# Ten units routed first, fourteen later, in a fused RWKV and mixture-of-experts kernel on one core

## The chip, the core and the metric

The kernel runs on one NeuronCore of a Trainium2 chip. The core has four compute engines that work side by side, each through its own queue in order: TensorE (PE, matrix products; PEld is its weight load), VectorE (DVE), ScalarE (ACT) and GpSimd (POOL). SyncE (SP) issues transfers. POOL can also issue an indirect transfer, which scatters the rows of a tile to row numbers held in another tile. The metric is device time in microseconds (us) of one execution, lower is better; a time is the median of several executions.

## What is computed

Attention first: a recurrence over 768 steps for 4 batches and 8 heads of size 48. Its output, 3072 rows of 384 numbers, goes through a mixture of 8 experts of which each row uses one.

```python
# attention, for each step t
cur = np.einsum('bhd,bhe->bhde', u[None] * kt, vt)
y[:, :, t] = np.einsum('bhd,bhde->bhe', rt, state + cur)
state = wt[:, :, :, None] * state + np.einsum('bhd,bhe->bhde', kt, vt)
# experts, x is y as (3072, 384)
logits = x @ w_gate + modality_bias[modality_id]
e_idx = np.argmax(logits, axis=1)
probs = softmax(logits); gate_w = probs[np.arange(N), e_idx]
h = np.maximum(x[mask] @ w1[e], 0.0)          # mask = e_idx == e
out[mask] = gate_w[mask, None] * (h @ w2[e])
```

The bias has a spread of 0.5 and the attention output is small, so in the given inputs nearly every row goes to the expert that the bias of its modality favours.

## The kernel before

**Attention.** The 3072 rows are 24 units of 128 rows (`NU`). One call of `att_iter(i)` is a turn; the loop at the end of the program runs i from -2 to 23. In turn i, DVE scans the decays of unit i+2 (`B`, `E`, L261 and L264) and masks the scores of unit i+1 (`A`, L303); POOL computes `dV` of unit i, `K` and `G` of unit i+2 (L268, L219, L272); PE makes the scores of unit i+1 (`pS`, L302) and the output of unit i (`pY`, L327 and L337). `x_rows` writes a finished unit to the tile `xp`, `x_cols` transposes it, and `logits` (L376) puts its 8 logits for each row into columns of `R`, one PSUM tile that also holds all scratch of the routing. Steps of setup and routing are put in a list, `hooks`; each turn takes one, after the logits of the turn and ahead of the matmuls of `pY`, but in turns 22 and 23 the logits are emitted after the hook, among or behind the matmuls of `pY`.

**Routing.** Units 0 to 11 are routed in turns 13 to 18 (`route_a`, `route_x`, `route_b`, then three steps of `table`). `route_a` finds the expert of each row, `route_b` counts ranks by matmuls and writes each row's place to `posT`; `scatter(n)` is then POOL's indirect write of unit n to `xs` in DRAM, where rows stand sorted by expert. `drain(2)` issues two of them behind each turn. `table` works out, for the first `NA` = 5 blocks of 256 rows, the expert, the place in `xs`, and whether the weights change. Units 12 to 23 are routed in blocks 0 and 1, written in blocks 2 and 3, and the second table holds the other `NB` = 7 blocks and halves.

**Blocks.** Weights of the expert that the bias favours (`e0`) are loaded and split in advance (`w_split_half`, POOL and ACT, turns 8 to 15). Each block q loads its rows by `blk_load` (SP, L576), which waits for all writes to `xs`; `blk_t` transposes them and splits them into `xh` and `xo` (L587 to L589); `blk_up` makes four groups of products with w1, `blk_down` four with w2, `blk_out` scales by the gate and writes the rows with POOL's indirect transfer (L627). `blk_t` of the next block stands in PE's queue between the ups and the downs of the present one. `w_split` splits the weights of the next block: w1 (DVE, ACT) in the ups, w2 (POOL, ACT) in the downs. `fetch` issues the load of block q+2 at the end of block q, for blocks from `NA` on; the loads of the first `NA` are issued in turn 21. Weights are loaded by a conditional transfer (`blk_raw`, L196), which moves nothing where the expert stays. Twelve blocks and one half block are laid out in the program; loops behind them take what overflows.

**Order.** The schedule is manual: each engine runs its instructions in the order in which the code emits them. What one engine writes and another reads or overwrites is guarded by semaphores that the framework places.

## Time and profile before

| | |
|---|---|
| median of 3 runs | 367.51 us (367.09 to 367.93) |
| the profiled execution | 367.16 us |
| its span, first to last instruction | 365.3 us |
| mean granted TensorE clock | 0.995 |
| PE, PEld busy | 349.1 us (96%), 334.6 us (92%) |
| DVE, ACT, POOL busy | 226.7 us (62%), 224.5 us (61%), 247.6 us (68%) |
| HBM traffic | 239 GB/s over the span |

Busy shares are means over two stages: the attention turns up to about 133 us, and the expert blocks behind them. PE's records are pipelined, so a busy PE is not PE at its peak. In a timeline row stand the start, the duration, the engine, the line, the operation with the tiles that it writes and reads, and, in brackets, the idle time ahead of it and what ended that.

### The profile page before, as it was taken

How to read it: one execution, taken by the hardware profiler on the slowest of the kernel's cores; microseconds unless marked ns; L12 is line 12 of the kernel's file. 1: busy time of each engine (PE TensorE's matmuls, PEld its weight loads, DVE VectorE, ACT ScalarE, POOL GpSimd, SP SyncE). 2: the span in 40 equal slices, each digit the busy share in tenths (PEclk: the TensorE clock that was granted, in tenths of full speed). 3: DMA queues.
4: the chain of work that ended last, by engine and by line, in shares of the span. 5: the costliest groups of instructions: out<-in, count | busy, mean ns of one | idle time of the engine just before them, and what ended most of it. 6: DMA issues, size and time to landing. Idle time of an engine off the chain costs nothing.

```text
span 365.3 us, 10829 instructions
## 1 busy us (share of the span) xinstructions
PE 349.1 (96%) x4245; PEld 334.6 (92%) x4245; DVE 226.7 (62%) x356; ACT 224.5 (61%) x466; POOL 247.6 (68%) x221
## 2 busy tenths in 40 slices
PE   7899999999898999999999999999999999999993
PEld 2788988998777999999999999999999999999992
DVE  6899999999998827671578390707161626661110
ACT  3665677677355538564586768686768585854340
POOL 5658868989798907856878867474747474728271
PEclk9999999999999999999999999999999999999998
DMA  8976887787795260012255613131222664065200
GB/s 283 330 200 196 247 217 230 229 233 214 199 282 167 70 216 1 2 45 65 108 184 188 209 52 109 50 104 57 96 72 82 185 234 154 20 215 155 81 26 26
DMA packets 20128, 53.28 MB, mean 146 GB/s; under 512 B 2693, under 2 KB 12587, under 8 KB 20068
## 3 DMA queue, kind: packets, MB, share of 16 engines
q1 hardware_dynamic: 16932, 43.04, 39.0%
q0 software_dynamic: 3136, 9.47, 6.9%
q8 instruction: 35, 0.57, 0.7%
q14 instruction: 25, 0.20, 0.2%
HBM read 75.66 MB, written 11.63 MB: 239 GB/s over the span
## 4 chain that ended last, share of the span: by engine, by line
PE 79%; DVE 9%; issue 6%; POOL 2%; ACT 1%; DMA 1%; POOLq 0%; DVEq 0%; ACTq 0%
PE pS_u L602 20%; PE pY_d L619 14%; PE pX_d L619 14%; PE pT_u L602 9%; PE pS L302 5%; PE pY L337 4%; PE pY L327 3%; DVE B L261 3%; DVE A L303 2%; PE pK L286 2%; PE pU_st L313 2%; DVE R L216 2%; PE pR_x L376 2%; PE pT L243 2%; PE pK_x L587 2%
## 5 line engine op out<-in xcount | busy, mean ns | idle before, releaser
L202 POOL TENSOR_TENSOR wl<-raw,wh 128x768 fp32r<-128x768 f32 x52 | 96.7, 1868 | 70.7 <-ACT wh L201 70.5
L201 ACT CAST wh<-raw 128x768 fp32r<-128x768 f32 x96 | 79.3, 830 | 34.1 <-PE pX_d L619 24.4
L602 PE MATMUL pS_u<-xh,wh 128*128 128x256 f32 x198 | 56.4, 285 | 0.0
L602 PE MATMUL pS_u<-xo,wh 128*128 128x256 f32 x198 | 55.9, 282 | 0.0
L602 PE MATMUL pS_u<-xh,wl 128*128 128x256 f32 x198 | 55.6, 281 | 0.0
L608 DVE SCALAR_TENSOR_TENSOR hl<-pS_u,hh 128x512 fp32r<-128x512 f32 x33 | 22.8, 690 | 52.7 <-ACT hh L607 51.2
L202 DVE TENSOR_TENSOR wl<-raw,wh 128x768 fp32r<-128x768 f32 x44 | 48.2, 1096 | 3.0 <-ACT wh L201 1.9
L627 POOL DMA_INDIRECT out<-ot,xl x25 | 32.6, 1302 | 10.9 <-ACT ot L626 5.3
L602 PEld LDWEIGHTS pS_u<-xh,wl 128*128 128x128 f32 x198 | 37.5, 190 | 0.0
L602 PEld LDWEIGHTS pS_u<-xh,wh 128*128 128x128 f32 x198 | 37.2, 188 | 0.0
L602 PEld LDWEIGHTS pS_u<-xo,wh 128*128 128x128 f32 x198 | 37.2, 188 | 0.0
L607 ACT ACTIVATE hh<-pS_u 128x512 fp32r<-128x512 f32 x33 | 19.7, 597 | 27.6 <-PE pS_u L602 22.9
L608 DVE SCALAR_TENSOR_TENSOR hl<-pT_u,hh 128x512 fp32r<-128x512 f32 x15 | 10.3, 690 | 40.8 <-ACT hh L607 40.3
L225 ACT ACTIVATE pU_st<-pU_st,B 128x48 f32<-128x48 f32 x80 | 22.0, 275 | 19.6 <-PE pU_st L313 13.8
L619 PE MATMUL pY_d<-wh,hh 128*128 128x384 f32 x96 | 33.6, 350 | 0.0
L619 PE MATMUL pY_d<-wh,hl 128*128 128x384 f32 x96 | 32.6, 339 | 0.0
L619 PE MATMUL pX_d<-wl,hh 128*128 128x384 f32 x96 | 32.6, 339 | 0.0
L619 PE MATMUL pX_d<-wh,hl 128*128 128x384 f32 x96 | 32.5, 338 | 0.0
L619 PE MATMUL pX_d<-wh,hh 128*128 128x384 f32 x96 | 32.5, 338 | 0.0
L619 PE MATMUL pY_d<-wl,hh 128*128 128x384 f32 x96 | 32.4, 338 | 0.0
L268 POOL TENSOR_TENSOR dV<-v,dT 128x384 f32<-128x384 f32 x24 | 20.0, 834 | 18.1 <-ACT dT L245 14.1
L303 DVE TENSOR_TENSOR A<-pS,cs 128x1024 f32<-128x1024 f32 x24 | 29.2, 1217 | 3.9 <-PE pS L302 2.0
(182 smaller groups left out, 899.6 us busy)
## 6 DMA issues: line engine op xcount, KB each, us to landing
raw<-w SPq DMA_DIRECT2D x52, 768.0 KB
in<-rkw SPq DMA_DIRECT2D x20, 674.2 KB
xl<-xs SPq DMA_DIRECT2D x12, 386.0 KB
v<-vt SPq DMA_DIRECT2D x24, 192.0 KB
wg<-wf SPq DMA_DIRECT2D x8, 576.0 KB
raw<-w SPq DMA_DIRECT2D x16, 192.0 KB
xs<-zt SPq DMA_DIRECT2D x8, 193.0 KB
in<-rkw SPq DMA_DIRECT2D x3, 512.0 KB
```

The costliest lines, as they stand in the source:

```text
L201: nc.scalar.copy(out=wh[k][:, sl], in_=raw[k][:, sl])
L202: (nc.vector, nc.gpsimd)[k].tensor_tensor(out=wl[k][:, sl], in0=raw[k][:, sl], in1=wh[k][:, sl].bitcast(F32), op=ALU.subtract)
L225: nc.scalar.activation(out=st[:, p], in_=st[:, p], func=AF.Copy, scale=tot[:, p, 0:1])
L268: nc.gpsimd.tensor_tensor(out=dV, in0=T["v", z].rearrange("p (a b) -> p a b", a=H), in1=T["dT", z].rearrange("p a b -> p (a b)")[:, :, Non ...
L302: nc.tensor.matmul(out=pS[:, hh, p], lhsT=K[q, p], rhs=R[q, p], start=True, stop=True)
L303: nc.vector.tensor_tensor(out=A.rearrange("p a b c -> p (a b) c"), in0=pS.rearrange("p a b c -> p (a b) c"), in1=mask[:, None, :].to_broad ...
L337: nc.tensor.matmul(out=pY[q:q + 64, h * D:(h + 1) * D], lhsT=A[:, hh, p, q:q + 64], rhs=v[:, h * D:(h + 1) * D], start=(first(z) and h == ...
L602: nc.tensor.matmul(out=pp[:, i], lhsT=wsrc[0][:, f, c * P:(c + 1) * P], rhs=xsrc[:, c], start=(n == 0), stop=(n == 3 * KC - 1))
L607: nc.scalar.activation(out=hh, in_=pp, func=AF.Relu)
L608: nc.vector.scalar_tensor_tensor(out=hl, in0=pp, scalar=0.0, in1=hh.bitcast(F32), op0=ALU.max, op1=ALU.subtract)
L619: nc.tensor.matmul(out=X["y", q][j], lhsT=hsrc[:, i, j * P:(j + 1) * P], rhs=wsrc[1][:, f], start=(f == 0 and n == 0), stop=(f == FC - 1 a ...
L627: ins = nc.gpsimd.indirect_dma_start(out=out[:, :], out_offset=bass.IndirectOffsetOnAxis(ap=xl[:, j, DM + 1:DM + 2].bitcast(I32), axis=0), ...
```

## The change

Units 0 to 9 are routed in turns 11 to 13 and units 10 to 23 in blocks 0 and 1 (`CUT`, `NJS`, `part`). `NA` becomes 4 and `NB` 8. Block 0 takes its expert and the place of its rows from `e0` (a new tile `e0r`), no longer from the table; its 256 rows are filled with padding first (a new transfer in turn 6), and the table takes off one block of that expert (`oh0`, `hd`). The first table's steps run in turns 22 and 23, two in each. `drain` issues one write a turn from turn 13 on, and two in turn 21, there between `K` and `G`. Only block 0 is loaded in turn 21, blocks 1 to 3 behind the last turn. Fourteen later writes go out in blocks 1 and 2; the second table's steps, the second `hook_b` and the padding rows move ahead by about a block. The bias is added to the logits by a matmul into `R` (`mfx`, `rbx`; one matmul with a start flag clears the tile first), so `route_a` has two operations fewer. The reciprocal of the gate's sum moves from `route_b` to `blk_t` and `half_t`. Sixteen half splits of w1 come ten in turns 8 to 12, three in turn 22 and three behind turn 23.

```diff
--- before.py
+++ after.py
@@ -28,8 +28,8 @@
 BT = 256
-NA = 5
-NB = 7
+NA = 4
+NB = 8
@@ -44,7 +44,8 @@
-NJ = 2 * NCH
+CUT = (0, 10, NU)
+NJS = (CUT[1], NU - CUT[1])
@@ -142,10 +143,16 @@
     e0f = cp.tile([P, 1], F32, name="e0f")
...
+    mfx = cp.tile([64, P], F32, name="mfx")
+    rbx = cp.tile([64, NU, E], F32, name="rbx")
+    mi2 = cp.tile([64, 2 * P], I32, name="mi2")
+    oh0 = cp.tile([P, E], F32, name="oh0")
+    e0r = cp.tile([P, 1], I32, name="e0r")
         nc.sync.dma_start(out=bb, in_=bass.AP(bias.tensor, bias.offset, [[0, P], [1, 2 * E]]))
         nc.sync.dma_start(out=mi, in_=mid)
+        nc.sync.dma_start(out=mi2[32:32 + NU], in_=mid)
     mf = raw[1][0:NU, 0, 0:P]
@@ -160,6 +167,12 @@
         nc.scalar.copy(out=mf, in_=mi[:, 0:2 * P:2])
         nc.scalar.copy(out=ersb[0:1], in_=ers[0:1])
         nc.scalar.copy(out=rcol(C_VEC + 3 * E, 1), in_=zt[:, 0:1])
+        nc.scalar.copy(out=mfx[0:NU], in_=mi[:, 0:2 * P:2])
+        nc.scalar.activation(out=mfx[32:32 + NU], in_=mi2[32:32 + NU, 0:2 * P:2], func=AF.Copy, scale=-1.0, bias=1.0)
+        for s in range(2):
+            q = slice(32 * s, 32 * s + NU)
+            nc.gpsimd.tensor_tensor(out=rbx[q], in0=ident[q, q, None].to_broadcast([NU, NU, E]),
+                                    in1=bb[q, None, (1 - s) * E:(2 - s) * E].to_broadcast([NU, NU, E]), op=ALU.mult)
@@ -172,14 +185,17 @@
     def setup_b():
-        pm = rcol(C_VEC, NU)
+        pm = T["pT", 5][:, 400:400 + NU]
         nc.tensor.transpose(out=pm, in_=mf, identity=ident[0:NU, 0:NU])
+        nc.tensor.matmul(out=T["R"][:, 0:NU * E], lhsT=mfx, rhs=rbx.rearrange("p a e -> p (a e)"), start=False, stop=True, skip_group_check=True)
         nc.scalar.copy(out=m1[:, 1], in_=pm)
         nc.gpsimd.tensor_scalar(out=m1[:, 0], in0=m1[:, 1], scalar1=-1.0, scalar2=1.0, op0=ALU.mult, op1=ALU.add)
         bias_part(0, biasT)
         nc.vector.tensor_reduce(out=e0f, in_=ec.rearrange("p a e -> p (a e)"), axis=AX.X, op=ALU.min)
+        nc.vector.tensor_scalar(out=oh0, in0=i8, scalar1=e0f[:, 0:1], scalar2=None, op0=ALU.is_equal)
         nc.gpsimd.tensor_scalar(out=e0f, in0=e0f, scalar1=float(E), scalar2=None, op0=ALU.add)
         nc.gpsimd.tensor_copy(out=e0i, in_=e0f)
+        nc.gpsimd.tensor_scalar(out=e0r, in0=e0f, scalar1=float(RS), scalar2=None, op0=ALU.mult)
@@ -248,7 +264,7 @@
     hooks = []
     done = iter(range(2 * FC))
-    SPLITS = {i: 2 for i in range(8, 16)}
+    SPLITS = {**{i: 2 for i in range(8, 13)}, 22: 3}
     def att_iter(i):
         a, m, z = i + 2, i + 1, i
@@ -269,6 +285,8 @@
                                     in1=T["dT", z].rearrange("p a b -> p (a b)")[:, :, None].to_broadcast([P, H, D]), op=ALU.mult)
         if ok(a):
             mk_k(a, k)
+            if i == NU - 3:
+                drain(2)
             nc.gpsimd.tensor_tensor(out=wt(a, "G", [P, 512]), in0=r, in1=k, op=ALU.mult)
         for _ in range(SPLITS.get(i, 0)):
             w_split_half(next(done))
@@ -352,29 +370,33 @@
...
     def x_rows(n):
...
-        if n % NJ == 0:
-
-            T["xp", b // 2] = (rt if b else xa).tile([P, NJ, XW], F32, tag="xp", name=f"xp{b}", bufs=1)
...
         if j == 0:
-            T["xb", b] = T["xp", b // 2][:, b % 2 * NCH:(b % 2 + 1) * NCH]
+
+            T["xp", c] = (rt if c else xa).tile([P, NJS[c], XW], F32, tag="xp", name=f"xp{c}", bufs=1)
         if n == 0:
             T["R"] = pt("x", "pR")
-        nc.vector.tensor_tensor(out=T["xb", b][:, j, 0:DM], in0=T["pY", n][:, 0:DM],
+
+            nc.tensor.matmul(out=T["R"][:, 511:512], lhsT=wm[:, 0:P], rhs=wm[:, 0:1], start=True, stop=True, skip_group_check=True)
+        nc.vector.tensor_tensor(out=T["xp", c][:, j, 0:DM], in0=T["pY", n][:, 0:DM],
                                 in1=T["dV", n].rearrange("p a b -> p (a b)"), op=ALU.add)
+    def part(n):
+        c = n >= CUT[1]
+        return int(c), n - CUT[c]
+
...
     def logits(n):
...
                 nc.tensor.matmul(out=T["R"][q:q + 64, n * E:(n + 1) * E], lhsT=T["xT", n][:, c * P + q:c * P + q + 64], rhs=wgs[:, c],
-                                 start=(c == 0), stop=(c == KC - 1), skip_group_check=True)
+                                 start=False, stop=(c == KC - 1), skip_group_check=True)
@@ -395,57 +416,58 @@
...
     def route_a(c):
...
-        nc.vector.scalar_tensor_tensor(out=lg, in0=lg, scalar=-1.0, in1=biasT[:, c * NJ:(c + 1) * NJ], op0=ALU.mult, op1=ALU.subtract)
...
-        nc.vector.tensor_reduce(out=mx, in_=lg, axis=AX.X, op=ALU.min)
-        nc.vector.tensor_tensor(out=eq, in0=lg, in1=mx[:, :, None].to_broadcast(sh), op=ALU.is_equal)
...
+        nc.vector.tensor_reduce(out=mx, in_=lg, axis=AX.X, op=ALU.max)
         nc.vector.tensor_tensor(out=lg, in0=lg, in1=mx[:, :, None].to_broadcast(sh), op=ALU.subtract)
         yield
-        nc.vector.tensor_tensor(out=eq, in0=eq, in1=i8[:, None, :].to_broadcast(sh), op=ALU.mult)
+        nc.vector.scalar_tensor_tensor(out=eq, in0=lg, scalar=0.0, in1=i8[:, None, :].to_broadcast(sh), op0=ALU.is_equal, op1=ALU.mult)
         nc.vector.tensor_reduce(out=ix, in_=eq, axis=AX.X, op=ALU.min)
...
         nc.vector.tensor_tensor(out=oh, in0=i8[:, None, :].to_broadcast(sh), in1=ix[:, :, None].to_broadcast(sh), op=ALU.is_equal)
         if c:
...
                 nc.vector.tensor_reduce(out=ohs, in_=T["oh", 0].rearrange("p a b -> p b a"), axis=AX.X, op=ALU.add)
-        nc.gpsimd.tensor_copy(out=T["xp", c][:, :, DM + 1:DM + 2].bitcast(I32), in_=tidi[:, c * NJ:(c + 1) * NJ, None])
+        nc.gpsimd.tensor_copy(out=T["xp", c][:, :, DM + 1:DM + 2].bitcast(I32), in_=tidi[:, CUT[c]:CUT[c + 1], None])
     def route_x(c):
...
-        nc.scalar.activation(out=ex, in_=rcol(c * NE, NJ, E), func=AF.Exp, scale=-1.0)
...
+        nc.scalar.activation(out=ex, in_=rcol(CUT[c] * E, NJS[c], E), func=AF.Exp)
         for n in (4, 2, 1):
             nc.gpsimd.tensor_tensor(out=ex[:, :, 0:n], in0=ex[:, :, 0:n], in1=ex[:, :, n:2 * n], op=ALU.add)
-        nc.gpsimd.tensor_scalar(out=ex[:, :, 0:1], in0=ex[:, :, 0:1], scalar1=1.0e-9, scalar2=None, op0=ALU.add)
+        nc.gpsimd.tensor_scalar(out=T["xp", c][:, :, DM:DM + 1], in0=ex[:, :, 0:1], scalar1=1.0e-9, scalar2=None, op0=ALU.add)
     def route_b(c):
...
-        add(pR[:, 0:NE], trib, oh.rearrange("p a b -> p (a b)"), True)
+        add(pR[:, 0:NE], trib, oh.rearrange("p a b -> p (a b)"), c == 1)
...
         if c:
...
-
-        for j in range(NJ):
-            add(pR[:, (j + 1) * E:], onesb, oh[:, j:j + 1].to_broadcast([P, NJ - j, E]), stop=j == NJ - 1)
...
+
+        for j in range(nj):
+            add(pR[:, (j + 1) * E:], onesb, oh[:, j:j + 1].to_broadcast([P, nj - j, E]), stop=j == nj - 1)
...
         nc.vector.tensor_tensor(out=rk, in0=rk, in1=oh, op=ALU.mult)
...
             nc.vector.tensor_reduce(out=po, in_=rk, axis=AX.X, op=ALU.add)
-        nc.vector.reciprocal(out=T["xp", c][:, :, DM:DM + 1], in_=T["ex", c][:, :, 0:1])
@@ -453,7 +475,7 @@
         vec, tt, ts = nc.vector, nc.vector.tensor_tensor, nc.vector.tensor_scalar
-        ct = rcol(C_RK + NE, E)
+        ct = rcol(C_RK + NJS[ph] * E, E)
...
@@ -492,7 +514,7 @@
             ts(out=es, in0=te, scalar1=float(E - 1), scalar2=None, op0=ALU.min)
             ts(out=tab[:, 0, o:o + nb], in0=te, scalar1=float(E - 1), scalar2=None, op0=ALU.min)
-            prev = e0f if o == 0 else tabe[:, o - 1:o] if o == NA else tabe[:, NQ - 1:NQ]
+            prev = e0f if o == 1 else tabe[:, o - 1:o] if o == NA else tabe[:, NQ - 1:NQ]
             for c0, c1, pv in ((0, 1, prev), (1, nb, es[:, 0:nb - 1])):
                 vec.scalar_tensor_tensor(out=tab[:, 2, o + c0:o + c1], in0=te[:, c0:c1], scalar=float(E - 1), in1=pv,
                                          op0=ALU.min, op1=ALU.not_equal)
@@ -502,12 +524,16 @@
...
         if ph == 0:
             rounded(g, ct, 1.0 / BT, -0.5 + 0.5 / BT)
+            hd = wt(ph, "hd", [P, E], 1)
+            tt(out=hd, in0=g, in1=oh0, op=ALU.min)
+            tt(out=g, in0=g, in1=hd, op=ALU.subtract)
             sums(cu, g)
-
-            ts(out=fs, in0=cu, scalar1=float(NA), scalar2=None, op0=ALU.min)
-            vec.scalar_tensor_tensor(out=fA, in0=cu[:, 1:E + 1], scalar=float(NA), in1=fs[:, 0:E], op0=ALU.min, op1=ALU.subtract)
             yield
-            yield from rows(0, NA, cu, fA, None)
+
+            ts(out=fs, in0=cu, scalar1=float(NA - 1), scalar2=None, op0=ALU.min)
+            vec.scalar_tensor_tensor(out=fA, in0=cu[:, 1:E + 1], scalar=float(NA - 1), in1=fs[:, 0:E], op0=ALU.min, op1=ALU.subtract)
+            yield from rows(1, NA - 1, cu, fA, hd)
+            tt(out=fA, in0=fA, in1=hd, op=ALU.add)
...
         vec.scalar_tensor_tensor(out=n, in0=fA, scalar=-float(BT), in1=ct, op0=ALU.mult, op1=ALU.add)
@@ -572,12 +598,13 @@
     def blk_load(q, at=None):
         at = q if at is None else at
         xl = bp["m"].tile([P, JT, XW], F32, tag="xl", name=f"xl{q}", bufs=5)
-        r = nc.sync.value_load(tab[0:1, 1, ds(at, 1)], min_val=0, max_val=DUMMY)
+        r = nc.sync.value_load(e0r[0:1, 0:1] if q == 0 else tab[0:1, 1, ds(at, 1)], min_val=0, max_val=DUMMY)
         nc.sync.dma_start(out=xl, in_=xs[ds(r, BT), :].rearrange("(j p) c -> p j c", p=P))
         X["xl", q] = xl
     def blk_t(q):
         xl = X["xl", q]
+        nc.vector.reciprocal(out=xl[:, :, DM:DM + 1], in_=xl[:, :, DM:DM + 1])
         xh = bp["m"].tile([P, KC, BT], F32R, tag="xh", name=f"xh{q}", bufs=2)
         for c0, c1, tg in ((0, 2, "pK"), (2, 3, "pU")):
@@ -639,6 +666,8 @@
         X["xl", q] = xl
     def half_t(q):
+        xl = X["xl", q]
+        nc.vector.reciprocal(out=xl[:, 0:1, DM:DM + 1], in_=xl[:, 0:1, DM:DM + 1])
         pp = pt(f"x{q}", tag="pK", sh=(P, KC, P))
         for c in range(KC):
             nc.tensor.transpose(out=pp[:, c], in_=X["xl", q][:, 0, c * P:(c + 1) * P], identity=ident)
@@ -682,9 +711,9 @@
     def hook_b(c):
...
-        pend.extend(range(c * NJ, (c + 1) * NJ))
-
-    for t, c in (*((t, 0.0) for t in SPb), (onesb, 1.0), (one8, 1.0), (ersb, 0.0), (zt, 0.0), (zt[:, DM + 1:DM + 2].bitcast(I32), PAD_ID),
+        pend.extend(range(CUT[c], CUT[c + 1]))
+
+    for t, c in (*((t, 0.0) for t in SPb), (onesb, 1.0), (one8, 1.0), (ersb, 0.0), (zt, 0.0), (zt[:, DM:DM + 1], 1.0), (zt[:, DM + 1:DM + 2].bitcast(I32), PAD_ID), (mfx, 0.0), (rbx, 0.0),
                  (glo, W_LO), (ghi, -W_HI)):
         nc.gpsimd.memset(t, c)
@@ -692,14 +721,18 @@
         if 6 <= i < 6 + 2 * FC:
             if i == 6:
                 e0 = nc.sync.value_load(e0i[0:1, 0:1], min_val=0, max_val=E - 1)
+                r0 = nc.sync.value_load(e0r[0:1, 0:1], min_val=0, max_val=(E - 1) * RS)
+                nc.sync.dma_start(out=xs[ds(r0, BT), :].rearrange("(j p) c -> p j c", p=P), in_=zt[:, None, :].to_broadcast([P, JT, XW]))
             w_raw(e0, (i - 6) // FC, (i - 6) % FC, parts=FC)
         if 3 <= i < 7:
             hooks.append((setup_a, setup_b, setup_c, setup_d)[i - 3])
-        if i == NJ + 1:
+        if i == CUT[1] + 1:
             ra, tb = route_a(0), table(0)
-            hooks.extend([lambda: next(ra), lambda: next(ra, None), lambda: hook_b(0), *[lambda: next(tb, None)] * 3])
-        if i == NJ + 2:
+            hooks.extend([lambda: next(ra), lambda: next(ra, None), lambda: hook_b(0)])
+        if i == CUT[1] + 2:
             route_x(0)
+        if i >= NU - 2:
+            hooks.append(lambda: [next(tb, None) for _ in range(2)])
         if i == NU - 1:
         att_iter(i)
@@ -713,15 +746,14 @@
         if i == 0:
             early()
-        drain(2)
-        if i == 19:
-            blk_raw(0, 0)
-            blk_raw(0, 1)
-        if i == 21:
-            for q in range(NA):
-                blk_load(q)
+        if i < NU - 3:
+            drain(1)
+        if i == NU - 3:
+            blk_load(0)
     assert not pend and not hooks
     blk_raw(1, 0)
+    for q in range(1, NA):
+        blk_load(q)
@@ -758,12 +790,15 @@
                 else:
                     logits(NU - 4 + g)
                 w_split(1, g)
-            if (q, g) == (1, 0):
-                route_x(1)
             if nxt < HO and g < late:
                 w_split(0, g)
-            if q in (2, 3):
+            if (q, g) == (1, 0):
+                hook_b(1)
+                tab1 = table(1)
+            if (q, g) > (1, 1):
                 drain(1)
+            if (q, g) == (2, 1):
+                next(tab1, None)
         if q == 0:
             blk_raw(1, 1)
         (blk_t if nxt < HO else half_t)(nxt)
@@ -771,26 +806,26 @@
             blk_raw(nxt2, 0)
         if 1 <= q <= NG:
             guard_load(q - 1)
-        if q == 1:
-            hook_b(1)
-        if q == 2:
-            tab1 = table(1)
         for g in range(FC // 2):
             blk_down(q, g)
             if q == 0 and g < FC // 2 - late:
                 w_split(0, late + g)
             w_split(1, g)
-            if q == 0 and g == FC // 2 - late:
+            if q == 0 and g == 0:
                 list(route_a(1))
+            if q == 0 and g == 1:
+                route_x(1)
             if g == 1 and 2 <= q <= NG + 1:
                 guard(q - 2)
-            if q == 2:
+            if q in (1, 2):
                 drain(1)
-
-            if (q, g) in ((2, 0), (2, 1), (2, 2), (3, 0), (3, 2)):
+            if q == 1:
                 next(tab1, None)
-            if (q, g) == (2, 0):
-                pad_rows()
+        if q == 1:
+            pad_rows()
+        if q == 2:
+            assert not pend
+            next(tab1, None)
         if q == 0:
             blk_raw(2, 0)
         if q == NG + 1:
```

## The prediction

> **What bounds the kernel now.** I read the chain of waits by engine first, then the windows by stage, then the timelines around the routing work. Times are on the before-trace's own clock.

> ```profile
> span 365.3 us, 10829 instructions
> PE 79%; DVE 9%; issue 6%; POOL 2%; ACT 1%; DMA 1%; POOLq 0%; DVEq 0%; ACTq 0%
> ```
> ```profile
> 76.40:110.00 33.60, 30.90 (x671) 27.83 (x670) 32.49 (x62) 19.36 (x59) 29.39 (x35) 1.00 0.81 232
> 207.40:340.00 132.60, 132.60 (x952) 132.44 (x952) 60.40 (x82) 90.89 (x143) 80.04 (x48) 1.00 0.36 117
> ```

> The columns after a stretch are its length and the busy time of PE, PEld, DVE, ACT and POOL. In the expert blocks (207.4 to 340 stands for them) PE is never idle: a microsecond of PE idleness there is a microsecond of span. In the attention turns (76.4 to 110) DVE is busy 32.49 of 33.60 us and POOL 29.39: there work taken from DVE or POOL shortens the span. So the change can win ahead of the blocks and lose wherever it makes PE wait.

> The seeded inputs, run through the reference, put 1336 of the first twelve units' rows on expert 1 (five full blocks), 1110 of the first ten's (four), 2663 and 409 of all on experts 1 and 6. Both kernels then run twelve blocks and one half with the same weight switches. No matmul of a block is saved.

> **Part 1, attention turns: -3.3 us.**

> ```profile
> 48.78 1.21 DVE L303 TENSOR_TENSOR A<-pS,cs 128x1024 f32<-128x1024 f32 x1
> 68.55 1.22 DVE L303 TENSOR_TENSOR A<-pS,cs 128x1024 f32<-128x1024 f32 x1
> 78.13 1.21 DVE L303 TENSOR_TENSOR A<-pS,cs 128x1024 f32<-128x1024 f32 x1
> 79.86 0.26 DVE L406 SCALAR_TENSOR_TENSOR pR_x<-pR_x,biasT 128x96 f32<-128x96 f32 x1
> 80.92 1.22 DVE L261 TENSOR_TENSOR_SCAN B<-in,pX_d 128x516 f32<-128x516 f32 x1
> 127.29 1.22 DVE L303 TENSOR_TENSOR A<-pS,cs 128x1024 f32<-128x1024 f32 x1 [0.90 <-PE pS L302]
> ```
> ```profile
> 98.77 1.01 POOL L558 DMA_INDIRECT xs<-xp,posT  x1 [0.17 <-DVE B L261]
> 100.08 0.97 POOL L558 DMA_INDIRECT xs<-xp,posT  x1 [0.30 <-issue]
> 104.45 1.00 POOL L558 DMA_INDIRECT xs<-xp,posT  x1 [0.17 <-issue]
> ```

> One A per turn: 48.78 is turn 7, 68.55 turn 11, 78.13 turn 13, 127.29 turn 22. Turns 7 to 13 take 29.35/6 = 4.89 us, turns 11 to 13 DVE's bare 4.79; turns 11 to 22 take 58.74/11 = 5.34. The excess has two causes. Four routing operations add 80.92 - 79.86 = 1.06 to a DVE that has no gap. And with two indirect writes POOL needs 104.45 - 98.77 = 5.68 a turn; one write is 1.31 of it, so the new turn needs 4.37, below DVE's 4.79. After the change eleven turns at 4.79 to 4.89 make 52.7 to 53.8, I take 53.3. What stays is two, three and two routing operations in turns 11 to 13, 7 x 0.23 = 1.6 (0.265 each for 96 columns, less for 80). 54.9 against 58.74 saves 3.8. From it goes what the bias costs in setup:

> ```profile
> 31.81 0.30 ACT L160 CAST raw<-mi 24x128 f32<-24x128 int32 x1
> ```

> The two new ACT copies are of this kind and stand ahead of a dT for which PE waits; pipelined, 0.2 each, they cost 0.4 (0 to 0.6), the bias matmul about 0.1. Net -3.3; ends -4.9 (all at 4.79, setup hidden) and -2.2 (a slow write or two as below).

> **Part 2, the table in the last two turns: +4.2 us.**

> ```profile
> L376 PEldq EVENT_SEMAPHORE  x6: 51/51/51, 82.5 to 111.1; - x6
> 128.36 0.47 PE L376 MATMUL pR_x<-cs,xT 128*64 128x8 f32 x12
> 133.17 0.49 PE L376 MATMUL pR_x<-cs,xT 128*64 128x8 f32 x12
> 133.59 0.39 PE L602 MATMUL pS_u<-xh,wh 128*128 128x256 f32 x1
> ```
> ```profile
> 102.60 0.20 DVE L474 TENSOR_TENSOR pR_x<-pR_x,cs 128x40 f32<-128x40 f32 x1
> 103.63 1.23 DVE L261 TENSOR_TENSOR_SCAN B<-in,pX_d 128x516 f32<-128x516 f32 x1
> 108.44 0.16 DVE L490 SCALAR_TENSOR_TENSOR pR_x<-pR_x,t2(0, 0)_1984 128x5 f32<-128x5 f32 x1
> 108.98 1.22 DVE L261 TENSOR_TENSOR_SCAN B<-in,pX_d 128x516 f32<-128x516 f32 x1
> 132.66 0.41 DVE L589 TENSOR_TENSOR xo<-pU_x,xh 128x256 fp32r<-128x256 f32 x1
> ```

> The first row decides. PE holds an extra wait ahead of the logits (L376) six times, from 82.5 to 111.1: turns 14 to 19, each the turn behind one of the six hooks in which DVE worked in the tile R. The logits write other columns of R than those hooks touch. So PE's writes to R stand behind DVE's earlier work on R, whatever the columns. Before, that cost nothing: the hook came behind its turn's logits and the next were a turn away. In turns 22 and 23 the code puts the logits behind the hook. Turn 22's hook is now 17 DVE operations (5 to the first yield, 12 to the second); five took 103.63 - 102.60 = 1.03, so 17 take 3.5. They start 1.14 after A (127.29), end 4.7 after it; the logits stood at 128.36, 1.07 after it: PE stalls 3.6. Turn 23's hook has 7: six took 0.54 and the last needs 0.15 to finish, so it ends 0.65 behind xo (133.07), at 133.7 against logits at 133.17: 0.6 more. Behind the waiting logits in PE's queue stand pY, delta, block 0's transposes and all blocks. Ends: 17 x 0.09 (the short six) gives 2.1 in all, 17 x 0.265 gives 5.1.

> [...]

> **Part 3, block 0's load: 0, behind part 2.**

> ```profile
> 126.56 5.67 SPq L576 DMA_DIRECT2D xl<-xs  x5
> 130.74 0.66 PE L587 MATMUL pK_x<-cs,xl 128*128 128x128 f32 x4
> 131.54 0.88 PE L327 MATMUL pY<-SPb,R 128*64 128x96 f32 x16
> 204.71 0.97 POOL L558 DMA_INDIRECT xs<-xp,posT  x1 [0.30 <-issue]
> 207.51 0.39 SPq L576 DMA_DIRECT2D xl<-xs  x1
> 208.50:210.50 2.00, 2.00 (x19) 2.00 (x18) 0.30 (x1) 1.69 (x4) 2.00 (x2) 1.00 0.73 198
> ```

> SP issues a load 2.80 after the start of the last write (204.71 to 207.51), and that load's traffic is over by 210.5: 3.0 more. (The load of 126.56 was there by 130.74, so at most 4.2; 1.0 passes before anything moves.) The two writes of turn 21 now go out between K and G, the second starting near 124.6; its load would be ready near 130.4 to 131.4 where PE wants it at 130.74. With PE 3.6 late it is hidden. If PE did not wait for the table, 1.1 would show: DVE's x_rows, 0.5 behind the table's end at 132.0, would release pY at 132.6 in place of 131.54.

> **Part 4, block 4's load: +5.3 us.** This is the price of routing fourteen units and four early blocks: the first load that waits for later writes is now issued one block earlier, with two writes more ahead of it.

> ```profile
> SPq L576 <- DMA xs<-xp,posT: 14.6, 2, 9.5
> 166.49 1.83 POOL L202 TENSOR_TENSOR wl<-raw,wh 128x768 fp32r<-128x768 f32 x1 [5.59 <-ACT wh L201]
> 184.98 1.85 POOL L202 TENSOR_TENSOR wl<-raw,wh 128x768 fp32r<-128x768 f32 x1 [2.12 <-ACT wh L201]
> 187.99 1.88 POOL L202 TENSOR_TENSOR wl<-raw,wh 128x768 fp32r<-128x768 f32 x1
> 198.25 0.44 PE pK_x L587 x4
> ```

> SP waited for these writes twice, once ahead of each batch of loads. Before, the late load was over at 210.5 and needed only after the ups of the block that begins at 207.4. Now it is needed one block earlier, at 198.25, in block 3. POOL's queue: two writes fit in the 5.59 idle ahead of 166.49. Then block 1's four pairs of weight split and write, 3.06 each (184.98 to 187.99, with gaps), end at 178.7; two output writes at 1.31 make it 181.3; four writes in block 2's ups, 186.5; four pairs, the last write starting at 197.7. Issue at 200.5, ready at 203.5: PE is 5.3 late. Ends: 3.5 (load in 2.0, no gaps) and 7.5 (three writes of 1.5 us, load in 4.2). Nothing can stand in: PE's queue is in order.

> **Part 5, the clock behind these stalls: +1.9 us.**

> ```profile
> 358.60 0.33 PE L667 MATMUL pY_d<-wh,hl 128*128 128x384 f32 x1
> 360.00:362.00 2.00, 0.00 (x0) 0.00 (x0) 0.00 (x0) 0.00 (x0) 0.84 (x1) 0.94 0.27 88
> 362.00:365.30 3.30, 0.00 (x0) 0.00 (x0) 0.00 (x0) 0.00 (x0) 0.00 (x0) 0.50 0.03 7
> ```
> ```profile
> 7.15 1.09 PE L286 MATMUL pK<-cs,K 128*128 128x128 f32 x4 [1.54 <-DVE R L216]
> 12.52 0.63 PE L286 MATMUL pK<-cs,K 128*128 128x128 f32 x4 [0.99 <-DVE R L216]
> ```

> The granted clock falls to 0.50 after the last matmul (358.93): 0.94 over two microseconds puts the fall at 361.8, 2.8 idle. At the start the same four transposes take 1.09, later 0.63: the way back to the full clock ends somewhere in those 5.4 us, so at most 2.7 is lost. A 5.3 us stall is long enough for the fall; I take half, 1.4. The 3.6 us stall is near the edge: 0.5 (0 to 1.5). [...]

> **At nothing.** Reciprocals move into each block ahead of xo, which waits for ACT anyway, while DVE has over half its time free (60.40 of 132.60); uncovered, thirteen at 0.16 (the row of 108.44) would be 2.1. The pad write to block 0's rows is issued in turn 6, fifteen turns ahead of its use; behind it and its register load on SP stand input loads that run turns ahead. Route 1's earlier place and the pad rows fall on free DVE and SP time. Block 1's conditional load follows the table by a microsecond or two; ACT needs it 3.5 after block 0 starts (cost 0, at worst 0.9).

> **Sum.** -3.3 + 4.2 + 0 + 5.3 + 1.9 = +8.1: span 373.4. Around the span lie 367.16 - 365.3 = 1.86, and the median (367.51) is 0.35 above the profiled run: 375.6, I say 375.5.

> **Rivals.** A, writes in time: if block 2's last write started by 192.5, block 4's load would be hidden, leaving -3.3 + 4.2 + 0.5 = +1.4: 368.9. For it: before, writes and load had room. Against: POOL's queue above has no slack. B, logits free of the table, load late: -3.3 + 1.1 + 5.3 + 1.4 = +4.5: 372.0. Against: the six waits. C, the other side, one mechanism: all order is kept by address, so that neither the logits wait for other columns of R nor a load for writes to other rows; -3.3 + 1.1 = -2.2: 365.3. It decides if both the six waits and SP's two have other causes. D, the reciprocal's strided column counts as overlapping the transposes' rows: each block's transposes then wait behind DVE's last split:

> ```profile
> 199.63 0.96 DVE L202 TENSOR_TENSOR wl<-raw,wh 128x768 fp32r<-128x768 f32 x1
> ```

> This split ends at 200.6, 2.3 after the transposes' 198.25; ten such blocks add 23, near 399. Against: columns and rows share no byte. That the change does nothing would need turns 11 to 22 to stay at 5.34; POOL's row speaks against it.

> **Chances.** Forecast 0.62 (its own range 373 to 379), A 0.12, B 0.12, C 0.10, D 0.04. The range 368.5 to 379 leaves out C, D, and the tails of A and the forecast. 0.2%, 0.7 us, is about what a measurement of this kernel can tell from no change. Faster: C with the low end of A, 0.11; within 0.04; slower 0.85.

> **What would show it.** Attention turns near 4.85 us from turn 14; PE idle about 3.5 us ahead of turn 22's logits, released by DVE's table; POOL's last row write after 195 and SP's load of block 4 behind it; PE idle about 5 us in block 3, then matmuls at half clock. Wrong if block 3 runs without a gap, or the six waits turn out to be something else.

## The result and the profile after

| | before | changed |
|---|---|---|
| device time, median | 367.30 us (366.92 to 367.93, 4 runs) | 384.02 us (382.75 to 388.40, 4 runs) |
| profiled execution | 367.16 us, span 365.3 | 385.15 us, span 383.3 |

The ratio is 1.0469, with a 95% interval of 1.0412 to 1.0527: 17 us slower, where 8 were forecast, and outside the range of 368.5 to 379. Sign and places were right, two sizes were not. Ratios leave out executions over 1.5% slower than the fastest of their kernel. First the head of the changed kernel's page (span, chain of waits by engine, granted clock in 40 slices), then PE's two longest waits (total, count, longest):

```profile
span 383.3 us, 10849 instructions
PEclk9999999999999759999998699999999999999999
PE 70%; POOL 9%; issue 9%; DVE 6%; DMA 3%; ACT 1%; POOLq 0%; DVEq 0%; ACTq 0%
```
```profile
PE pK_x L614 <- DMA xl<-xs: 8.4, 1, 8.4
PE pR_x L398 <- DVE t2(0, 1)_2473 L509: 3.6, 1, 3.6
```

PE's share of the chain fell from 79% to 70%. The two waits are the ones that the prediction named, and nothing like them stood in the kernel before. The clock has two dips, one behind each. The tail of the attention phase, in the changed kernel's timeline (A of turn 22, the table's last operation in that turn, the logits, the first up):

```profile
124.96 1.23 DVE L321 TENSOR_TENSOR A<-pS,cs 128x1024 f32<-128x1024 f32 x1 [0.89 <-PE pS L320]
129.50 0.16 DVE L509 TENSOR_TENSOR t2(0, 1)_2473<-pR_x,t2(0, 1)_2473 128x3 f32<-128x3 f32 x1
129.80 0.81 PE L398 MATMUL pR_x<-cs,xT 128*64 128x8 f32 x12 [3.60 <-DVE t2(0, 1)_2473 L509]
139.25 0.58 PE L629 MATMUL pS_u<-xh,wh 128*128 128x256 f32 x1
143.25 0.49 PE L392 MATMUL pT_('x', 0)_2688<-cs,xp 128*128 128x128 f32 x3
```

Before, A began at 127.29, these logits at 128.36, the first up at 133.59. A is 2.33 us earlier. From A to logits took 1.07 and takes 4.84; from logits to first up 5.23 and now 9.45, with the same matmuls and no wait among them; the 18 matmuls of the first up took 2.26 (133.59 to 135.85) and now 4.00. The windows around the two dips (PE, PEld, DVE, ACT, POOL busy, then the granted clock, where 1.00 is full speed and 0.50 half, DMA share, GB/s) say why:

```profile
126.20:129.60 3.40, 0.00 (x0) 0.00 (x0) 2.85 (x17) 0.00 (x0) 1.12 (x3) 1.00 0.38 116
129.60:143.25 13.65, 13.45 (x147) 12.75 (x148) 2.39 (x12) 2.26 (x7) 2.52 (x4) 0.50 0.12 33
143.25:146.65 3.40, 3.40 (x30) 3.40 (x30) 1.81 (x3) 3.15 (x6) 1.34 (x1) 1.00 0.73 231
204.70:208.10 3.40, 1.08 (x10) 0.87 (x8) 3.37 (x3) 1.60 (x3) 3.21 (x3) 1.00 0.16 58
208.10:218.35 10.25, 4.12 (x15) 4.12 (x16) 2.35 (x5) 0.86 (x2) 2.69 (x3) 0.50 0.59 179
218.35:221.75 3.40, 3.40 (x20) 3.40 (x20) 0.00 (x0) 1.28 (x2) 1.66 (x1) 1.00 0.12 44
```

The wait of 3.6 us was followed by 13.65 us at half clock, although PE was busy for 13.45 of them. And block 4's load, from the last row writes to the transposes that it holds up in block 3 (POOL, SP, PE):

```profile
185.16 1.53 POOL L584 DMA_INDIRECT xs<-xp,posT  x1 [0.17 <-DMA raw<-w]
188.44 1.73 POOL L654 DMA_INDIRECT out<-ot,xl  x1 [0.31 <-issue]
203.59 1.53 POOL L584 DMA_INDIRECT xs<-xp,posT  x1 [0.17 <-issue]
207.13 1.53 POOL L584 DMA_INDIRECT xs<-xp,posT  x1 [0.17 <-issue]
210.42 0.39 SPq L602 DMA_DIRECT2D xl<-xs  x1
214.23 1.12 PE L614 MATMUL pK_x<-cs,xl 128*128 128x128 f32 x4 [8.45 <-DMA xl<-xs]
```

Span against span, stage by stage, with the prediction's terms beside (all on the profiled executions):

| stage | predicted | measured | from |
|---|---|---|---|
| attention up to A of turn 22 | -3.3 | -2.33 | 124.96 against 127.29 |
| table's hold on the logits | +4.2 | +3.77 | 4.84 against 1.07; none in turn 23 |
| half clock behind it | +0.5 | +5.96 | 9.45 - 5.23, and 4.00 - 2.26 |
| blocks 0 to 3 up to the wait, rest | 0 | +0.13 | 66.53 against 64.66, less 1.74 |
| wait for block 4's load | +5.3 | +8.45 | the row of 214.23 |
| half clock behind it | +1.4 | +2.02 | 169.07 from there to the end against 167.05 |
| sum | +8.1 | +18.0 | 383.3 - 365.3 |

The wait begins at 205.78, 66.53 behind the first up; before, those transposes began at 198.25, 64.66 behind it. Not all of the 5.96 is the clock: with the clock at full speed in the same stretch (f2_filler, below), logits to first up still take 5.81, 0.58 over the kernel before, so some 5.4 are the clock's.

### The profile page after: what moved, and what is told of

Read it like the earlier page. It is cut to its first block, busy times and chain, and to the rows that moved or that the text cites. A ratio compares the mean times of both kernels' runs of the same rounds, so it can differ in the third digit from the quotient of the medians.

```text
span 383.3 us, 10849 instructions
## 1 busy us (share of the span) xinstructions
PE 355.9 (93%) x4248; PEld 341.5 (89%) x4248; DVE 229.9 (60%) x372; ACT 225.6 (59%) x468; POOL 252.1 (66%) x227
## 4 chain that ended last, share of the span: by engine, by line
PE 70%; POOL 9%; issue 9%; DVE 6%; DMA 3%; ACT 1%; POOLq 0%; DVEq 0%; ACTq 0%
PE pS_u L629 15%; PE pY_d L646 11%; PE pX_d L646 11%; PE pT_u L629 6%; PE pS L320 6%; PE pY L355 5%; POOL wl L218 3%; POOL xs L584 3%; PE pY L345 3%; PE pK L304 2%; PE pU_st L331 2%; POOL out L654 2%; PE pT L259 2%; DVE B L277 2%; PE pR_x L398 2%
## 5 line engine op out<-in xcount | busy, mean ns | idle before, releaser
L629 PE MATMUL pS_u<-xh,wh 128*128 128x256 f32 x198 | 57.2, 289 | 0.0
L629 PE MATMUL pS_u<-xo,wh 128*128 128x256 f32 x198 | 56.7, 286 | 0.0
L629 PE MATMUL pS_u<-xh,wl 128*128 128x256 f32 x198 | 56.4, 285 | 0.0
L218 DVE TENSOR_TENSOR wl<-raw,wh 128x768 fp32r<-128x768 f32 x44 | 50.0, 1136 | 1.7 <-ACT wh L217 0.7
L654 POOL DMA_INDIRECT out<-ot,xl x25 | 34.2, 1369 | 11.0 <-ACT ot L653 5.3
L629 PEld LDWEIGHTS pS_u<-xh,wl 128*128 128x128 f32 x198 | 38.3, 194 | 0.0
L629 PEld LDWEIGHTS pS_u<-xo,wh 128*128 128x128 f32 x198 | 38.0, 192 | 0.0
L629 PEld LDWEIGHTS pS_u<-xh,wh 128*128 128x128 f32 x198 | 38.0, 192 | 0.0
L584 POOL DMA_INDIRECT xs<-xp,posT x24 | 26.5, 1103 | 6.6 <-issue 4.2
L290 POOL TENSOR_TENSOR G<-in 128x512 f32<-128x512 f32 x24 | 30.8, 1283 | 0.0
```

Source lines behind the costliest of these rows:

```text
L218: (nc.vector, nc.gpsimd)[k].tensor_tensor(out=wl[k][:, sl], in0=raw[k][:, sl], in1=wh[k][:, sl].bitcast(F32), op=ALU.subtract)
L290: nc.gpsimd.tensor_tensor(out=wt(a, "G", [P, 512]), in0=r, in1=k, op=ALU.mult)
L584: rows_apart("xs", nc.gpsimd.indirect_dma_start(out=xs[:, :], out_offset=bass.IndirectOffsetOnAxis(ap=posT[:, n:n + 1], axis=0), in_=T["xp ...
L629: nc.tensor.matmul(out=pp[:, i], lhsT=wsrc[0][:, f, c * P:(c + 1) * P], rhs=xsrc[:, c], start=(n == 0), stop=(n == 3 * KC - 1))
L654: ins = nc.gpsimd.indirect_dma_start(out=out[:, :], out_offset=bass.IndirectOffsetOnAxis(ap=xl[:, j, DM + 1:DM + 2].bitcast(I32), axis=0), ...
```

## The experiments

Theory: the loss is these two waits and the clock behind them, and each can be taken out alone. Rivals: the tail is slow for another reason than the clock; the logits or the load wait for something else; the two losses are one.

**Without the idleness (f1_filler).** Ahead of the logits of turn 22:

```diff
+                for _ in range(52):
+                    nc.tensor.matmul(out=pY[:, 384:512], lhsT=wm[:, 0:P], rhs=wm[:, 0:P], start=True, stop=True, ...)
                 logits(z - 2)
```

> The changed kernel, with 52 matmuls of 128x128 zeros (bf16) that nobody reads put into PE's queue ahead of the logits of turn 22, where PE idled 3.60 us. They leave the wait as it is and take only the idleness away. Theory (clock): of the 9.7 us that the wait costs, 3.7 are the wait and 6.0 the clock: from logits to first up 9.45 us in place of 5.23, and 18 ups 4.00 in place of 2.26. The granted clock stays 1.00 from 126 to 143 and the time is 384.0 - 6.0 = 378 us. Rival (the tail is slow for another reason: the operands come late, or DMA traffic): the same matmuls stay at half speed and the time stays at 384.

Measured: ratio to before 1.0285 (1.0247 to 1.0322), that is 377.5 us, as expected. The filler stands between pY's two halves, in pY's own tile and with the start flag set, and this kernel leaves out a part of the result (a relative error of 0.041). The author took the part to be unit 22's first half, the product with the state; no run shows which it is. The profiled execution, one of 383.22 us, had the tail at full clock (10.65 us from A to first up, 14.29 in the changed kernel), but lost the clock elsewhere, in turn 4; its windows there, and PE's wait in the first of them:

```profile
31.75:35.15 3.40, 2.37 (x45) 1.99 (x43) 2.86 (x5) 2.40 (x9) 2.37 (x6) 0.99 0.52 133
35.15:48.75 13.60, 13.60 (x177) 12.52 (x174) 9.41 (x13) 3.63 (x11) 6.28 (x11) 0.50 0.53 175
```
```profile
33.18 0.55 PE L393 MATMUL pT<-cs,xp 128*128 128x128 f32 x3 [1.03 <-ACT dT L261]
```

One microsecond of idleness, in a window with PE 70% busy, was followed by 13.6 us at half clock. The changed kernel has the same wait, in a window with PE 70% busy too (2.37 of 3.41 us, 30.59 to 34.00), and kept its clock there.

**The same, with pY whole (f2_filler).** The filler stands ahead of pY's first half.

> The changed kernel, with 52 matmuls of 128x128 zeros (bf16) that nobody reads put into PE's queue in turn 22 ahead of pY's first half, so that PE is idle for some 0.6 us in place of 3.60 ahead of the logits. The wait itself stays: the logits still start when the table's 17 operations end, some 4.8 us behind A. Theory (clock): the half clock that followed this wait goes (in the changed kernel's trace from 129.6 to 143.3 us, 6.0 us longer than at full clock), so 384.0 - 6.0 = 378 us; the granted clock is 1.00 from A of turn 22 to the first ups. Rival (the tail is slow for another reason than the clock): the chain from logits to first up stays near 9.45 us and the time at 384.

Measured: 384.23 us, ratio 1.0454 (1.0415 to 1.0494). The time missed, the clock did not. Window, then timeline of f2_filler:

```profile
126.00:143.00 17.00, 15.83 (x278) 14.90 (x278) 7.97 (x32) 5.21 (x15) 5.99 (x9) 1.00 0.16 40
```
```profile
128.29 1.23 DVE L321 TENSOR_TENSOR A<-pS,cs 128x1024 f32<-128x1024 f32 x1 [0.90 <-PE pS L320]
128.55 3.07 PE L344 MATMUL pY<-wm 128*128 128x128 bf16 x52
133.13 0.52 PE L401 MATMUL pR_x<-cs,xT 128*64 128x8 f32 x12 [0.70 <-DVE t2(0, 1)_2473 L512]
138.94 0.39 PE L632 MATMUL pS_u<-xh,wh 128*128 128x256 f32 x1
```

The logits still start 4.84 us behind A, but PE now idles 0.70, the clock stays at 1.00, and logits to first up take 5.81 in place of 9.45. So the half clock in the tail was the work of the idleness. What hid the gain: A of turn 22 comes at 128.29, 3.33 later than in the changed kernel, because turns 17 to 22 took 5.09 to 5.37 us, where the changed kernel takes 4.8 and, in turn 22, 3.96. (A turn's time is taken here from the A of the turn before to its own.) This slower pace came again in r1_dense and v1_setup; what starts it stays open (below).

**Dense work behind the fall (r1_dense).** 64 matmuls of zeros behind the logits, into pT's free columns.

> The changed kernel, with 64 matmuls of 128x128 zeros (bf16) that nobody reads behind the logits of turn 22, where the clock has just fallen; they cost 3.6 us at full and 6.8 at half clock. In the traces so far every stretch at half clock lasted 3.4, 6.8, 10.2 or 13.6 us, and PE was busy all through them with the attention's small tiles (64 columns or 64 rows). Theory (a window of 3.41 us brings the clock back only if the array's work in it is dense): the fall comes as before and the clock is back within two windows, 6.8 us, of the fall, in or right behind these matmuls, in place of 13.7; from there transposes, pY and ups run at full clock: 384.0 + 6.8 - 6.0 = about 385 (383 to 387). Rival (any busy window brings it back, or a fixed time does): half clock goes on to about 13.7 us behind the fall, and the time is 390.

Measured, in one execution: 391.76 us. The windows of r1_dense, and its dense stretch:

```profile
133.45:136.85 3.40, 0.57 (x14) 0.58 (x15) 2.27 (x13) 0.00 (x0) 0.00 (x0) 1.00 0.01 3
136.85:140.25 3.40, 3.40 (x34) 3.40 (x33) 0.00 (x0) 0.00 (x0) 0.00 (x0) 0.50 0.02 5
140.25:147.25 7.00, 6.68 (x150) 6.18 (x148) 2.33 (x11) 2.26 (x7) 2.33 (x4) 1.00 0.01 2
```
```profile
136.73 5.37 PE L351 MATMUL pT<-wm 128*128 128x128 bf16 x64
```

The clock fell after the wait as before and was back after a single 3.4 us of dense matmuls; the same small tiles then ran at full speed (1.00 from 140.25 to 147.25, pY's second half 1.14 and 1.09 us). The forecast of the time missed by nearly 7 us for another reason: A of turn 22 came at 131.43, 6.47 late. That is the slower pace and one more fall of the clock, from 95.90 to 102.73, in which turns 16 and 17 took 7.04 and 6.35 us.

**Logits ahead of the table (t1_logits_first).** In turns 22 and 23:

```diff
-        if hooks:
+        if hooks and i < NU - 2:
             hooks.pop(0)()
...
                 logits(z - 2)
+                hooks.pop(0)()
...
         if i == NU - 1:
             logits(z - 2)
+            hooks.pop(0)()
```

> The changed kernel, with the table's two hooks issued behind the logits of turns 22 and 23 in place of ahead of them; no instruction more or less. Theory (PE waits for DVE's table in the tile R, whatever the columns, and the clock falls in that wait): the wait of 3.6 us and the 6.0 of half clock go; DVE's x_rows then stands behind the table's 17 operations, up to 1.9 us late, of which about 1.3 reach PE: 384.0 - 3.6 - 6.0 + 1.3 = 375.7 us. Rival (the logits are late for their own operand, xT): 384 as before. Rival (order matters but the clock has another cause): 384.0 - 3.6 + 1.3 = 381.7.

Measured: 378.84 us, ratio 1.0290 (1.0233 to 1.0347): 5.2 us gained, 8.3 expected. The wait of 3.6 us is gone, x_rows behind the table costs the 1.0 that rival B reckoned as 1.1, and the clock fell again, for half as long; timeline and windows of t1_logits_first:

```profile
129.65 1.06 PE L345 MATMUL pY<-SPb,R 128*64 128x96 f32 x16 [1.01 <-DVE xp L383]
```
```profile
126.85:130.25 3.40, 2.07 (x44) 1.77 (x42) 3.06 (x15) 1.78 (x6) 1.43 (x3) 0.99 0.08 26
130.25:137.05 6.80, 6.80 (x71) 6.78 (x68) 1.00 (x9) 0.00 (x0) 1.09 (x2) 0.50 0.01 2
```

No idleness here lasted over 1.01 us; PE was 61% busy in the window. So a fall does not take one long wait.

**Late writes earlier (w1_early_writes).**

```diff
             if (q, g) > (1, 1):
-                drain(1)
+                drain(2 if q == 1 or g < 2 else 1)
```

> The changed kernel, with the fourteen late row writes issued two at a time in block 1's last two ups and block 2's first two ups (4 + 4 + 6 in place of 2 + 4 + 4 + 4), so that none stands between POOL's weight splits of block 2's downs. Theory (block 4's load is late because the last row write is the eighth of a POOL queue without slack): two writes go into POOL's idle 171.3 to 174.0, four leave the splits' queue; the last write starts near 197 in place of 207.1, the load lands 7.1 later, near 204, before PE asks for it at 205.8. The stall of 8.45 us and 2.0 of half clock behind it go: 384.0 - 10.4 = 373.6 us. Rival (the load waits for something else, SP's queue or the table): stall and time stay, 384. Rival (half clock behind the stall has another cause): 375.6.

Measured: 370.43 us, ratio 1.0093 (1.0064 to 1.0123). Last row write, load and block 3's transposes in w1_early_writes:

```profile
194.83 0.98 POOL L584 DMA_INDIRECT xs<-xp,posT  x1 [0.30 <-issue]
197.45 0.39 SPq L602 DMA_DIRECT2D xl<-xs  x1
203.42 0.60 PE L614 MATMUL pK_x<-cs,xl 128*128 128x128 f32 x4
```

The wait is gone, and the half clock behind it. The 3 us beyond the expectation lie in the tail: the fall after the table's wait lasted 6.8 us here (130.88 to 137.71), not 13.65. The work behind the wait was the same as in the changed kernel, and the clock was back before the first up (138.81).

**Both (c1_both, c1_again).** The two edits, with only five of the table's operations in turn 22 and the other 19 behind block 0's split of x:

```diff
-            hooks.append(lambda: [next(tb, None) for _ in range(2)])
+            hooks.append(lambda n=1 if i == NU - 2 else 3: [next(tb, None) for _ in range(n)])
```

> Both edits at once, with the table's second and third part (19 operations) behind block 0's split of x in turn 23, where DVE is free until the first hl, and only its first 5 operations in turn 22. Theory: the two costs are separate and both go wholly, 384.0 - 9.7 - 10.4 = 364 us (363.5 to 366), which is under the kernel before (367.3). Rival (they share something: with PE earlier by 9.7 us, POOL's writes, which are not paced by PE alone, come late again): block 3 waits again, 367 or more.

> c1_both once more, to narrow its interval: 364.6 us (363.5 to 365.5) against 367.0 to 367.7 of the kernel before; turns 15 to 21 at 4.79 us.

Measured: 364.62 us, ratio 0.9949 (0.9912 to 0.9987), and 364.59, ratio 0.9954 (0.9927 to 0.9982). The losses were separate and both went: in both profiled executions neither wait is left, nor a fall of the clock between 16.1 us and the last matmuls. With them out, the change's own gain shows: 0.5% under the kernel before.

**Two writes a turn again (a1_two_writes).** c1_both with `drain(2)` in the turns:

> c1_both with two indirect writes a turn in turns 14 to 18 in place of one in turns 14 to 20 and so on: the change's 'one write a unit' undone alone. Theory (POOL's second write set the pace of the turns before): POOL needs 5.68 us a turn with two writes, 4.37 with one, DVE 4.79; the five turns with two writes take 5.68 each, 0.89 over 4.79: A of turn 22 comes 4.4 us later than 53.5 behind A of turn 11, and the time is 364.6 + 4.4 = 369. Rival (the routing operations on DVE set the pace, or the writes hide): the turns stay at 4.79 and the time at 364.6.

Measured: 367.80 us, ratio 1.0029 (0.9994 to 1.0064). From A of turn 11 to A of turn 22 it takes 57.52 us (70.26 to 127.78), in c1_both 53.48 (69.23 to 122.71): 4.04 for the second write, close to the 4.4 from POOL's row. With it undone the kernel is no faster than before, so the net gain hangs on this part of the change.

**Setup (v1_setup, v2_copies, v3_pad12).** In the changed kernel ACT's two new copies stand ahead of dT, for which PE waits in turn 4:

```profile
32.64 0.30 ACT L170 CAST mfx<-mi 24x128 f32<-24x128 int32 x1
32.97 0.31 ACT L171 ACTIVATE mfx<-mi 24x128 f32<-24x128 int32 x1
33.30 0.17 ACT L261 COPY dT<-pT 128x8 f32<-128x8 f32 x1
33.52 0.55 PE L392 MATMUL pT<-cs,xp 128*128 128x128 f32 x3 [1.04 <-ACT dT L261]
35.21 1.23 DVE L321 TENSOR_TENSOR A<-pS,cs 128x1024 f32<-128x1024 f32 x1 [0.47 <-PE pS L320]
37.14 0.40 DVE L195 TENSOR_SCALAR oh<-cs,e0f 128x8 f32<-128x8 f32 x1
```

Turn 4 takes 5.65 us there, 5.08 before. Turn 5 takes 5.31 and 4.87; the last row is why, more than the bias matmul: the new `oh0` is one operation more on DVE, which has no idle time in that turn, and from A to the scan `B` DVE takes 2.25 us (35.21 to 37.46) in place of 1.81. v2_copies moves the copies to POOL, v3_pad12 the write of padding from turn 6 to turn 12, v1_setup both.

```diff
-        nc.scalar.copy(out=mfx[0:NU], in_=mi[:, 0:2 * P:2])
-        nc.scalar.activation(out=mfx[32:32 + NU], in_=mi2[32:32 + NU, 0:2 * P:2], func=AF.Copy, scale=-1.0, bias=1.0)
+        nc.gpsimd.tensor_copy(out=mfx[0:NU], in_=mi[:, 0:2 * P:2])
+        nc.gpsimd.tensor_scalar(out=mfx[32:32 + NU], in0=mi2[32:32 + NU, 0:2 * P:2], scalar1=-1.0, scalar2=1.0, op0=ALU.mult, op1=ALU.add)
```

> c1_both with the two new copies of setup (mfx) on POOL in place of ACT, and the write of padding to block 0's rows issued in turn 12 in place of turn 6. Theory (ACT's two copies stand ahead of the dT copy that PE waits for, 0.63 us, and cost turn 4 its 0.57): turn 4 takes 5.08 us in place of 5.65. Theory for the pad write (its 0.4 MB stand in the queues ahead of the instructions that PE fetches): turn 8 takes at most 5.05 in place of 5.46. Both: 364.6 - 1.0 = 363.6 us. Rival: turn 4 stays (the copy of dT waits for POOL) and the stall of turn 8 is there or elsewhere whatever the pad write: 364.6.

> c1_both with only the two mfx copies on POOL in place of ACT; the write of padding stays in turn 6. In v1_setup turn 4 took 5.09 us as expected, but turns 15 to 22 took 5.07 to 5.83 in place of 4.79, and the time was 367.7. Theory (the pad write of turn 12 did that): turn 4 at 5.09, turns 15 to 21 at 4.79, time 364.6 - 0.6 = 364.0 us. Rival (the copies moved the engines against each other and that did it): turns 16 to 22 above 5.05, time 367.5.

> c1_both with only the write of padding to block 0's rows moved from turn 6 to turn 12. Theory (its traffic delays turn 15, and the turns behind it keep the slower pace): turns 15 to 22 above 5.05 us, time 367.5. Rival (the copies did it): turns 15 to 21 at 4.79, time 364.6.

Measured: v1_setup 367.70 us, ratio 1.0002 (0.9978 to 1.0027); v2_copies 363.18, 0.9890 (0.9862 to 0.9918); v3_pad12 364.57, 0.9940 (0.9907 to 0.9972). With the copies on POOL turn 4 took 5.14 us, and v2_copies is the fastest here, 1.1% under the kernel before, its six runs within 1.1 us (362.67 to 363.79). Its A of turn 22 and first up:

```profile
122.61 1.23 DVE L321 TENSOR_TENSOR A<-pS,cs 128x1024 f32<-128x1024 f32 x1 [0.89 <-PE pS L320]
129.23 0.39 PE L631 MATMUL pS_u<-xh,wh 128*128 128x256 f32 x1
```

A is 4.68 us ahead of before, the first up 4.36, the span (360.9) 4.4. No cost of the write of padding in turn 6 shows: without it there, turn 8 took 6.00 us in v3_pad12, with it 5.46 in c1_both and 5.17 in c1_again. Neither move alone starts the slower pace of v1_setup (turns 15 to 22 at 5.07 to 5.83). There ACT's dT copies come late behind the matmuls that they read and PE waits for them: the copy of 90.29 began 1.13 us behind the end of its matmuls, and from 84 to 115 PE waited 2.1 us in four turns of six, in c1_both 0.3 in one. What holds ACT there no view shows, and it stays open. The chip is a rival that was not tested: the three kernels with the slower pace ran on one chip, v2_copies and v3_pad12 on another. On the chip of the three, a1_two_writes still took 4.80 in turns 19 and 20, so the chip alone does not do it.

## Why the prediction was right or wrong

- **Part 5, the clock, is the step that failed.** It took the loss from the way back, "at most 2.7", called turn 22's wait "near the edge", and put 0.5 there and 1.4 behind block 4. Both were the author's estimates; that 3.6 us lies near an edge no run shows: the clock fell behind idleness of 1.01 us (t1_logits_first) and of 3.60. Measured: 5.96 (some 5.4 of it the clock) and 2.02, 6.1 us of the 9.9 by which the sum was short. Wrong was that the way back takes a fixed short time. Half clock lasted 13.65 us, three steps of 3.41 us with the attention's small tiles and one filled by block 0's ups; f2_filler kept the clock up and took the tail's 3.6 off, r1_dense had it back after 3.4 us. That the small tiles are why it took so long is not shown: the same tiles had the clock back after two steps in w1_early_writes (130.88 to 137.71), and tiles like them after one in c1_again (12.68 to 16.09). Behind block 4's wait, with dense matmuls, it was back 4.1 us after the first of them, and 2.02 is close to 1.4. The half-clock stretches here lasted 3.4, 6.8, 10.25 and 13.65 us, one to four steps of 3.41. A busy PE alone did not end them: in the 13.65 us it was busy for 13.45.
- **Part 4, block 4's load, was right as a mechanism and too small:** 8.45 for 5.3, outside its ends. The blocks ran 7.5 us behind the kernel before (139.25 - 133.59, and 66.53 - 64.66), so the last write, put at 197.7, was due at 205.2; it began at 207.13. Five indirect writes of 1.14 to 1.73 us, where 1.0 was reckoned, account for those 1.9. From there to the issue took 3.29 (2.80 reckoned), to the transposes 3.81 (3.0 reckoned): 1.3 more. That there was no slack in POOL's queue was right, and w1_early_writes, which moves only writes in this queue, has no such wait. Rival A needed the slack and fell.
- **Part 2, the table, was right:** 3.60 of idleness for 3.6. The 0.6 in turn 23 did not show, as PE came late by the clock; in f2_filler, with the clock up, it was 0.32. t1_logits_first shows that place in the queue decides, although the columns are apart, and gives rival B's price, 1.0 for 1.1. By what rule the logits wait for other columns of R was not shown. Rival C fell with both waits.
- **Part 1, attention:** -2.33 for -3.3, within its ends only just. Turns 11 to 22 gained more than reckoned (54.02 for 58.74, -4.72 where -3.8 was put). Setup cost more: A of turn 11 came 2.39 later, not 0.5. The two misses have opposite signs; that their sum stayed inside the ends is luck. Turn 4 gave 0.57, for the two ACT copies, which took 0.33 each and not 0.2 (with them on POOL 0.51 of it went). Turn 5 gave 0.44, for `oh0`, which the sum had left out. Turn 8 gave 0.89 of the remaining 1.38: PE stalled there for 1.11 us with nothing that the profile shows as releaser, and such stalls moved from kernel to kernel (the longest 1.2 in c1_again and v3_pad12, 0.7 in w1_early_writes, 0.4 in v2_copies).
- **Part 3 and the edits at nothing** held but for `oh0`: blocks 0 to 3 were 0.13 longer apart from the clock, and the reciprocals, the pad rows and block 1's load do not appear. Rival D did not happen.

With part 5 at its measured value the sum would have been +14.2 (381.7 us), still above the range; with part 4's too, +17.3 of the +18.0.

## What to carry to other kernels

A wait of PE is priced with the work that follows it: behind it the clock may fall, and the half clock can then cost more than the wait (5.4 us against 3.6 here). A step moved into the last turns of a stage belongs behind that stage's last matmuls in program order, even where engine time is free, if it works in a tile that those matmuls also write (here 17 operations of DVE on R held the logits for 3.60 us, and with the logits ahead of them, in t1_logits_first, this wait was gone). When work is cut anew between two phases, count the slots of the slowest queue up to the first consumer: here two writes in each of four slots took away a wait of 8.45 us and the half clock behind it.
